# Three groups' first parts are added later on VectorE, their output transfers behind that, and four more blank products run at the start

## The chip, the cores and the metric

The kernel runs on one core of one Trainium2 chip. The metric is the device time of one execution in microseconds, as the median of several runs. The core has five engines that run their own queues in order and wait for each other by semaphores: TensorE (matrix products, PE in the profile), VectorE (DVE), ScalarE (ACT), GpSimd (POOL) and SyncE (SP, which here only starts transfers). A transfer is started by an instruction in one engine's queue and then runs on the DMA engines.

## The reference

An mLSTM cell over 4 batches, 8 heads, 768 steps and 40 features is followed by a feed-forward block on its output, seen as 3072 tokens of 320 features:

```python
for t in range(S):
    m_new = np.maximum(f_gate[:, :, t] + m, i_gate[:, :, t])
    f_stab = np.exp(f_gate[:, :, t] + m - m_new)
    i_stab = np.exp(i_gate[:, :, t] - m_new)
    C = f_stab * C + i_stab * outer(v[t], k[t])
    n = f_stab * n + i_stab * k[t]
    y[:, :, t] = sigmoid(o_gate[t]) * (C @ q[t]) / np.maximum(np.abs(n . q[t]), 1.0)
x = y as (3072, 320)
h = x @ w_in            # 320 -> 2048
g = h - np.tanh(h)
out = g @ w_out         # 2048 -> 320
```

## The kernel before

The sequence is cut into 24 units (6 chunks of 128 steps for each of 4 batches). Two units form a group of 256 tokens, so there are 12 groups, and the feed-forward block works on groups. The 2048 hidden features are 8 pairs of 256 (`p` from 0 to 7). An *item* is one or two pairs of one group: up products into PSUM banks (`ph_up`), then the function g as a polynomial, its *cubes* and products on VectorE with squares on ScalarE, then down products.

**Order.** Every engine's instructions keep the order in which the program issues them (`Pinned`, `T`). The first items are laid out by a planner; from item 7 (`START`) on, a loop lays out one item after another. In it a program clock (`Clock`, line 135) advances by a fixed cost for each product (0.218 for an up product, 0.27 for a down product), and `Clock.later(key, wait, step)` issues a step at the first advance that has passed its due time. This clock only sets the order of the program; it measures nothing.

**Up products in seven.** `up_in_seven` (line 1221) replaces eight block products by seven, on sums of weights and sums of x. Two PSUM banks X and Y hold the partial results; Y's halves are `b` and `e`, X's are `a` and one shared by `c` and `d`. In the order of TensorE: stage one (four products), three down products of an earlier item, stage two (two products), three more down products, stage three (eight products), then the quarter products of the last 64 features. ScalarE copies halves between the products: `b` from `a` and `cs` from `c` behind stage one, `d` from `b` behind stage two, `e` from `b` behind the first product of stage three. The last product of stage three, `w(3)` by `s4`, adds onto `b`. `shrunk` (line 1265) then issues, for ScalarE, a square of `b`, a square of `a`, `q`, `z` and `q`; for VectorE two sums `both` (of `d` and `e` with `cs`) and two cubes. The second `both` waits for the square of `b`. The cubes free the banks for the next item. Behind `shrunk`, by the clock, follow further products, and 3.4 later the sums `s` for the down products (`sums_of_g`, line 1017).

**Put-together.** Down products in seven (`down_seven`, line 1030) collect in PSUM banks `pS`. When a group is done, `put_together` (line 1073) lets ScalarE copy one block (`a`), and its inner `rest` (line 1083), 0.5 later, builds the output tile `ob` on VectorE in four sums. The pairs 0 to 3 of groups 0, 1 and 2 (`g < FIRST`) were done earlier in another way, and their result lies in `parts_of[g]` (128 by 640 numbers); for those, `rest` adds it in a fifth instruction (line 1090). Then the transfer of `ob` to `out` goes into ScalarE's queue, 2.0 later (line 1094).

**Part sums.** `sum_w_in(p)` (line 1197) builds three blocks of sums of weights on GpSimd. For pairs 0, 1 and 2 they are written over `parts_of[p]`, so after that group's add. They are placed at 4.05, 6.05 and 8.05 items behind `START` (line 1737) and are read by the up products of later items (`ph_up<-xT,part`).

**Blank products.** While TensorE has nothing to do at the start, `idle` (line 1698) fills the time with products of a constant into an unused bank (`awake`, line 428). The first stretch, before the first gate transposes, holds ten.

Of the kernel before, what the change touches and what calls it, by code (L numbers as in the profile page):

```python
# [55 lines left out]
OP = mybir.AluOpType  # L56
# [23 lines left out]
def kernel(  # L80
# [33 lines left out]
    V, A, SP, G = Pinned(nc.vector), Pinned(nc.scalar), Pinned(nc.sync), Pinned(nc.gpsimd)  # L114
# [42 lines left out]
    class Plan:  # L157
# [45 lines left out]
        def flow(cls, moved):  # L203
# [22 lines left out]
            return ends  # L226

        def run(self, idle, fill):
            while self.todo:
                ready = [(t, op) for op in self.todo if (t := self.start(op)) is not None]  # L230
# [23 lines left out]
                if op["engine"] == "T":  # L254
                    n = idle(self.free["T"], t)
                    self.done.append((t - n, t, 1.0))
                    us = us * (self.COLD[1] if t < self.COLD[0] else 1.0) + self.TURN * (op["tiles"] != self.tiles)
                    self.tiles = op["tiles"]
                    self.done.append((t, t + us, op["dense"]))
# [21 lines left out]
    GT = 2  # L281
# [12 lines left out]
    FIRST, SPLIT = 3, 4  # L294
# [112 lines left out]
    two = const.tile([128, 1], FP, name="two")  # L407
# [20 lines left out]
    def awake(n):  # L428

        if not spare:  # L430
            spare.append(ps_o.tile([128, 512], FP, name="awake", tag="po1"))
        stream(spare[0], n)

    def stream(bank, n):
        for _ in range(n):
            T.matmul(bank.rearrange("p (h t) -> p h t", h=HH), diag[:, 0], diag[:, 0:1].to_broadcast([128, HH, L]), start=True, stop=True)
# [204 lines left out]
    parts_of = [const.tile([L, GT, DM], FP, name=f"part{g}") for g in range(NP // 2)]  # L641
# [431 lines left out]
    def put_together(g):  # L1073
        bank = pS[g]

        ob = mlp.tile([128, 5, HM], FP, name="ob", tag="ob")
        a = mlp.tile([128, HM], FP, name="a", tag="a", bufs=1)
        u = mlp.tile([128, 2, HM], FP, name="u", tag="u", bufs=1)

        def twice(t):  # L1080
            return t.unsqueeze(1).to_broadcast([128, 2, HM])

        def rest():
            V.tensor_tensor(out=ob[:, 0:5:4], in0=bank[0][:, 0:2], in1=twice(a), op=OP.add)
            V.tensor_tensor(out=u, in0=bank[1], in1=twice(ob[:, 4]), op=OP.add)
            V.tensor_tensor(out=ob[:, 3], in0=bank[1][:, 0], in1=u[:, 1], op=OP.add)
            V.tensor_tensor(out=ob[:, 1:3], in0=bank[2], in1=u, op=OP.add)
            if g < FIRST:
                both = ob[:, 0:2 * GT]
                V.tensor_tensor(out=both, in0=both, in1=parts_of[g].rearrange("p t (two n) -> p (t two) n", two=2), op=OP.add)  # L1090
            c, b = divmod(g * GT, B)
            rows = out.rearrange("(b c t) n -> c t b n", b=B, c=NT)[c][:, b:b + GT]
            whole = ob[:, 0:4].rearrange("p (t two) n -> p t (two n)", two=2)
            Clock.later("sent", 2.0, lambda: A.dma_start(out=rows, in_=whole))

        if g in third:
            return lambda: A.copy(out=a, in_=bank[0][:, 2]), rest
        A.copy(out=a, in_=bank[0][:, 2])
        Clock.later("result", 0.5, rest)
# [97 lines left out]
    def sum_w_in(p, E=V):  # L1197

        a11, a21, a12, a22 = (w_in[:, p, i * 128:(i + 1) * 128] for i in range(4))
        t = sums_in_of(p)  # L1200
        both = w_in[:, p, 0:4 * 128].rearrange("p (j f) -> p j f", j=4)
        return [lambda: E.tensor_tensor(out=t[:, 0:4:2], in0=both[:, 1:4:2], in1=both[:, 0:2], op=OP.subtract),
                lambda: E.tensor_tensor(out=t[:, 1], in0=a22, in1=t[:, 0], op=OP.subtract),
                lambda: E.tensor_tensor(out=t[:, 3], in0=a12, in1=t[:, 1], op=OP.subtract)]
# [196 lines left out]
    while sum(map(len, items)) < len(pairs):  # L1401
        x = sum(map(len, items))
# [18 lines left out]
    plan = Plan(small=("b0", "b1"), a=1, up=1, po0=1, po1=1, gt=2, z=1, s4=1, P=4, vs=4, w64a=2, w64b=2, w=2, wm=2, ob=2)  # L1421
# [45 lines left out]
    of_tokens, of_states, exponentials, rows = {}, {}, [], []  # L1467
# [230 lines left out]
    def idle(t0, t1, share=0.9):  # L1698


        one = 0.43 if t0 < plan.COLD[0] else 0.217
        n = int((t1 - t0) * (1.0 if t0 < plan.COLD[0] else share if t0 > 18.0 or share == 1.0 else 0.65) / one)
        if n and not busy:
            awake(n)
        else:
            pool, tag = next(((pool, tag) for name, pool, tag in (("a", ps_a, "a0"), ("up", ps_h, "ph0"), ("po0", ps_o, "po0"), ("po1", ps_o, "po1"))
                              if plan.tokens[name] and plan.tokens[name][0][0] <= t0), (None, None))
            if n and pool:
                stream(pool.tile([128, 512], FP, name="awake", tag=tag), n)
            else:  # L1710
                n = 0
        return n * one

    plan.run(idle, lambda t0, t1: idle(t0, max(t1, t0 + 0.25), 1.0))


# [3 lines left out]
    def spread_over(steps, x0, x1):  # L1720

        for i, (cost, step) in enumerate(steps):
            at = x0 + i * (x1 - x0) / len(steps)
            work[int(at)].append((at, cost, step))
# [9 lines left out]
    for i, slot in enumerate(slots):  # L1734
        x0, x1 = (START + max(0, 2 * j - 1) for j in (i, i + 1))
        begins[x0].append((slot, x0, x1))
    for p, x in enumerate((4.05, 6.05, 8.05, 2.02, 0.5, 0.8, 1.1, 1.3)):
        spread_over([(0.0, lambda step=step: step()) for step in sum_w_in(p, G)], START + x, START + x + 0.25)
    late = (4, 0.0, V), (5, 0.04, G), (6, 0.95, V), (7, 0.3, G)
    for p, x, E in (*late, *((p, x, G) for p, x in zip(order_of(FIRST)[:2] + order_of(FIRST)[-2:], (1.5, 1.75, 6.6, 7.5)))):  # L1740
# [158 lines left out]
    with tc.If(loaded[0] > 0):  # L1899
# [21 lines left out]
        for g in range(NG):  # L1921
# [18 lines left out]
            ob = [ps_o.tile([128, DM], FP, name="po", tag=f"po{tt}") for tt in range(GT)]  # L1940
# [56 lines left out]
```

## Time and profile before

| what | value |
|---|---|
| median of 3 runs | 492.97 us (492.12 to 493.79) |
| profiled execution | 492.58 us |
| its span, first to last instruction | 490.9 us |
| busy: TensorE, VectorE, ScalarE, GpSimd | 480.2, 409.8, 268.9, 125.3 us |
| mean granted TensorE clock | 0.998 |

Times in rows are microseconds from the start of the span, unless marked ns. In a timeline a row is one instruction or a run of like ones (x4) with its start and length; the brackets give the idle time of the engine before it and what ended that. The ends of products on TensorE are modelled and overlap the next start.

### The profile page before, as it was taken

The page shows a single profiled execution, that of the slowest core. Times are in us where ns is not written, and L with a number is a line of the kernel's source. Part 1 is how long each engine was busy: PE and PEld are TensorE (multiplying, and loading weights), DVE is VectorE, ACT ScalarE, POOL GpSimd, SP SyncE. Part 2 cuts the span into 40 slices and gives each one's busy share as a digit, 9 for nine tenths or more (in the row PEclk, how much of TensorE's full clock was granted, in tenths as well). Part 3 has the DMA queues.
Part 4 walks back from the last instruction along what each step waited for, and adds up shares of the span by engine and source line. Part 5 has one row for each costly group of instructions (what it writes and reads, how often), then busy time and mean ns, then how long its engine had stood idle before and what let it go on. Part 6 is the DMA issues. An engine that isn't in the chain of part 4 may idle for free.

```text
span 490.9 us, 13826 instructions
## 1 busy us (share of the span) xinstructions
PE 480.2 (98%) x5208; PEld 432.5 (88%) x5208; DVE 409.8 (83%) x966; ACT 268.9 (55%) x729; POOL 125.3 (26%) x248
## 2 busy tenths in 40 slices
PE   8999999999899999999999999999999999999995
PEld 4778877789798899999999999999999999998985
DVE  4899989998999997987988888888888888885853
ACT  4888978534445444544644554555455554555540
POOL 5642325827431711111111111102102111111000
PEclk9999999999999999999999999999999999999999
DMA  7996585223635544535544435445345343320001
GB/s 222 308 257 188 75 165 160 72 51 90 144 78 124 114 92 109 115 75 115 109 96 101 97 95 106 103 93 115 68 102 115 79 96 54 65 59 9 28 2 33
DMA packets 140077, 51.27 MB, mean 104 GB/s; under 512 B 119908, under 2 KB 132388, under 8 KB 140004
## 3 DMA queue, kind: packets, MB, share of 16 engines
q1 hardware_dynamic: 131084, 31.18, 31.4%
q0 software_dynamic: 5440, 15.05, 10.6%
q10 hardware_dynamic: 3480, 4.10, 2.5%
q8 instruction: 43, 0.70, 0.6%
q14 instruction: 30, 0.25, 0.2%
HBM read 38.40 MB, written 11.60 MB: 102 GB/s over the span
## 4 chain that ended last, share of the span: by engine, by line
PE 89%; DVE 7%; issue 2%; ACT 1%; DMA 0%; SPq 0%; ACTq 0%; DVEq 0%
PE ph_up L129 39%; PE pS L129 31%; PE po L129 5%; PE pT L129 4%; PE ps L129 3%; PE pc L129 2%; PE ph L129 2%; DVE gt L106 1%; PE awake L129 1%; DVE ob L106 1%; DVE s L106 1%; ACT z L106 1%; DMA w_out<-in_i_gate 0%; DVE both L106 0%; PE px L133 0%
## 5 line engine op out<-in xcount | busy, mean ns | idle before, releaser
L129 PE MATMUL ph_up<-xT,w_in 64*64 64x256 f32 (+3 forms) x1324 | 155.0, 349 | 0.0
L129 PEld LDWEIGHTS ph_up<-xT,w_in 128*128 128x128 f32 (+2 forms) x1324 | 114.0, 162 | 17.2 <-issue 3.3
L106 ACT ACTIVATE z<-ph_up 128x256 f32<-128x256 f32 (+1 forms) x98 | 40.6, 416 | 98.0 <-PE ph_up L129 83.8
L106 POOL DMA_DIRECT2D xT<-y_rows x54 | 31.6, 590 | 238.5 <-DMA y_rows<-yt 218.5
L106 ACT COPY ph_up<-ph_up 128x256 f32<-128x256 f32 x117 | 41.8, 357 | 92.0 <-PE ph_up L129 58.4
L129 PE MATMUL pS<-wT,s 128*128 128x160 f32 x504 | 86.7, 300 | 0.0
L129 PEld LDWEIGHTS pS<-wT,s 128*128 128x128 f32 x504 | 72.9, 191 | 0.3 <-issue 0.3
L106 ACT ACTIVATE q<-z,tiny 128x512 f32<-128x512 f32 (+1 forms) x98 | 68.9, 713 | 2.5
L106 DVE SCALAR_TENSOR_TENSOR gt<-q,gt 128x512 f32<-128x512 f32 (+1 forms) x98 | 66.3, 683 | 3.7 <-ACT q L106 1.2
L106 DVE TENSOR_TENSOR both<-ph_up,cs 128x256 f32<-128x256 f32 x78 | 32.8, 422 | 37.6 <-PE ph_up L129 32.2
L129 PE MATMUL pS<-w_out,gt 128*128 128x160 f32 x336 | 56.9, 312 | 0.0
L129 PE MATMUL ph_up<-xT,sums_in 128*128 128x128 f32 x336 | 51.6, 276 | 2.2 <-DVE gt L106 2.2
L129 PEld LDWEIGHTS pS<-w_out,gt 128*128 128x128 f32 x336 | 46.8, 189 | 4.4 <-issue 1.9
L129 PEld LDWEIGHTS ph_up<-xT,sums_in 128*128 128x128 f32 x336 | 45.5, 191 | 3.2 <-issue 2.6
L129 PE MATMUL ph_up<-xT,part 128*128 128x128 f32 x288 | 44.7, 278 | 1.1 <-DVE gt L106 0.9
L106 DVE SCALAR_TENSOR_TENSOR gt<-ph_up,z 128x256 f32<-128x256 f32 (+1 forms) x98 | 41.1, 457 | 2.3 <-ACT z L106 2.2
L129 PEld LDWEIGHTS ph_up<-xT,part 128*128 128x128 f32 x288 | 38.9, 191 | 2.9 <-ACT ph_up L106 1.8
L106 DVE TENSOR_TENSOR s<-gt 128x256 f32<-128x256 f32 x84 | 33.1, 434 | 1.4
L129 PE MATMUL pS<-wT,gt 128*128 128x160 f32 x168 | 29.8, 300 | 0.0
L129 PE MATMUL pS<-w_out,s 128*128 128x160 f32 x168 | 29.7, 299 | 0.0
L129 PE MATMUL po<-w_out,gt 128*128 128x320 f32 x96 | 27.9, 439 | 0.0
L106 DVE SCALAR_TENSOR_TENSOR gt<-both,z 128x512 f32<-128x512 f32 x39 | 26.6, 683 | 0.0
(141 smaller groups left out, 738.2 us busy)
## 6 DMA issues: line engine op xcount, KB each, us to landing
w<-in_moe_w_out POOLq DMA_DIRECT2D x8, 640.0 KB, 6.1
h_rows<-zt SPq DMA_DIRECT2D x68, 64.0 KB
z_in<-h_rows SPq DMA_DIRECT2D x68, 64.0 KB
w<-in_moe_w_in POOLq DMA_DIRECT2D x16, 256.0 KB, 6.3
kz<-in_kT SPq DMA_DIRECT2D x48, 80.0 KB
o<-in_o_gate SPq DMA_DIRECT2D x24, 160.0 KB
qz<-in_qT SPq DMA_DIRECT2D x44, 80.0 KB
out<-ob ACTq DMA_DIRECT2D x11, 320.0 KB
```

Source lines behind the costliest of these rows:

```text
L106: i = method(*args, **kwargs)
L129: return cls.keep(nc.tensor.matmul(*args, **kwargs))
```

## The change

It does three things. The add of the parts of groups 0, 1 and 2 becomes a step of its own, `add_parts`, due 6.0 after `rest` on the program's clock, and their output transfer is due 1.0 after that; the other groups keep theirs. The first blank stretch gets four more products. The part sums of pairs 0, 1 and 2 move back by 0.2 of an item, so that they are issued after the add that reads what they overwrite.

```diff
@@ put_together, rest @@
             V.tensor_tensor(out=ob[:, 1:3], in0=bank[2], in1=u, op=OP.add)
-            if g < FIRST:
-                both = ob[:, 0:2 * GT]
-                V.tensor_tensor(out=both, in0=both, in1=parts_of[g].rearrange("p t (two n) -> p (t two) n", two=2), op=OP.add)
             c, b = divmod(g * GT, B)
             rows = out.rearrange("(b c t) n -> c t b n", b=B, c=NT)[c][:, b:b + GT]
             whole = ob[:, 0:4].rearrange("p (t two) n -> p t (two n)", two=2)
-            Clock.later("sent", 2.0, lambda: A.dma_start(out=rows, in_=whole))
+
+            def add_parts():
+                both = ob[:, 0:2 * GT]
+                V.tensor_tensor(out=both, in0=both, in1=parts_of[g].rearrange("p t (two n) -> p (t two) n", two=2), op=OP.add)
+                Clock.later("sent", 1.0, lambda: A.dma_start(out=rows, in_=whole))
+
+            if g < FIRST:
+                Clock.later("sent", 6.0, add_parts)
+            else:
+                Clock.later("sent", 2.0, lambda: A.dma_start(out=rows, in_=whole))
@@ idle @@
-            awake(n)
+            awake(n + 4 if t0 < plan.COLD[0] else n)
@@ places of sum_w_in @@
-    for p, x in enumerate((4.05, 6.05, 8.05, 2.02, 0.5, 0.8, 1.1, 1.3)):
+    for p, x in enumerate((4.25, 6.25, 8.25, 2.02, 0.5, 0.8, 1.1, 1.3)):
```

## Rows read from the trace of the kernel before

**Rows 1.** The page, chain of work that ended last, shares by engine.

```profile
PE 89%; DVE 7%; issue 2%; ACT 1%; DMA 0%; SPq 0%; ACTq 0%; DVEq 0%
```

**Rows 2.** Waits of TensorE: who waited for whom, us in total, times, longest.

```profile
PE ph_up L129 <- DVE gt L106: 3.1, 3, 1.8
...
PE ph_up L129 <- ACT ph_up L106: 0.2, 1, 0.2
```

**Rows 3.** TensorE's timeline: start, us, what, idle before; the three restarts and `w(3)` products.

```profile
130.20 0.68 PE L129 MATMUL ph_up<-xT,sums_in 128*128 128x128 f32 x4 [1.77 <-DVE gt L106]
...
134.58 1.63 PE L129 MATMUL ph_up<-xT,w_in 128*128 128x128 f32 x20
...
150.23 0.68 PE L129 MATMUL ph_up<-xT,part 128*128 128x128 f32 x4 [0.91 <-DVE gt L106]
...
154.62 1.63 PE L129 MATMUL ph_up<-xT,w_in 128*128 128x128 f32 x20
...
169.76 0.68 PE L129 MATMUL ph_up<-xT,sums_in 128*128 128x128 f32 x4 [0.40 <-DVE gt L106]
...
174.23 1.63 PE L129 MATMUL ph_up<-xT,w_in 128*128 128x128 f32 x20
```

**Rows 4.** VectorE's timeline behind group 0's put-together, and group 2's add.

```profile
127.06 0.82 DVE L106 TENSOR_TENSOR ob<-ob,part 128x640 f32<-128x640 f32 x1
127.80 0.48 DVE L106 TENSOR_TENSOR vs<-v,crossed 128x320 f32<-128x320 f32 x1
...
128.97 0.42 DVE L106 TENSOR_TENSOR both<-ph_up,cs 128x256 f32<-128x256 f32 x1 [0.35 <-ACT z L106]
129.31 0.75 DVE L106 SCALAR_TENSOR_TENSOR gt<-ph_up,z 128x256 f32<-128x256 f32 x2
...
166.47 1.03 DVE L106 TENSOR_TENSOR ob<-ob,part 128x640 f32<-128x640 f32 x1
```

**Rows 5.** ScalarE's timeline: group 0's transfer, the next square, the copy `e` from `b`.

```profile
127.92 0.44 ACTq L106 DMA_DIRECT2D out<-ob  x1
128.46 0.38 ACT L106 ACTIVATE z<-ph_up 128x256 f32<-128x256 f32 x1 [4.72 <-DVE vs L106]
...
133.89 0.36 ACT L106 COPY ph_up<-ph_up 128x256 f32<-128x256 f32 x1 [0.86 <-PE ph_up L129]
```

**Rows 6.** Timelines of ScalarE and VectorE, one item later: squares and sums `both`.

```profile
136.37 0.38 ACT L106 ACTIVATE z<-ph_up 128x256 f32<-128x256 f32 x1 [2.12 <-PE ph_up L129]
...
137.64 0.71 DVE L106 TENSOR_TENSOR both<-ph_up,cs 128x256 f32<-128x256 f32 x2
...
156.40 0.38 ACT L106 ACTIVATE z<-ph_up 128x256 f32<-128x256 f32 x1 [2.12 <-PE ph_up L129]
...
156.54 0.79 DVE L106 TENSOR_TENSOR both<-ph_up,cs 128x256 f32<-128x256 f32 x2
```

**Rows 7.** VectorE's timeline: the last of the sums `s` behind group 1's put-together.

```profile
154.59 0.43 DVE L106 TENSOR_TENSOR s<-gt,s 128x256 f32<-128x256 f32 x1
```

**Rows 8.** Timelines of GpSimd and VectorE: part sums of pair 0, sums `s`.

```profile
133.02 1.16 POOL L106 TENSOR_TENSOR part<-w_in 128x256 f32<-128x256 f32 x1
134.26 1.11 POOL L106 TENSOR_TENSOR part<-w_in,part 128x128 f32<-128x128 f32 x2
...
133.64 1.42 DVE L106 TENSOR_TENSOR s<-gt 128x256 f32<-128x256 f32 x2
```

**Rows 9.** Timeline of TensorE's products (PE) and loads (PEld) in the first 12 us.

```profile
1.14 3.86 PE L129 MATMUL awake<-diag 128*128 128x512 bf16 x10 [1.14 <-DVE probe L106]
...
3.67 0.15 PEld L129 LDWEIGHTS <-diag 128*128 128x128 bf16 x1 [0.28 <-issue]
...
4.10 0.15 PEld L129 LDWEIGHTS <-diag 128*128 128x128 bf16 x1 [0.28 <-issue]
...
5.46 0.28 PE L133 MATMUL gate<-ident,w_in 32*128 32x32 f32 x2 [0.46 <-DVE w_in L106]
...
7.51 1.24 PE L129 MATMUL awake<-diag 128*128 128x512 bf16 x5
...
9.78 2.12 PE L129 MATMUL awake<-diag 128*128 128x512 bf16 x9
```

## The prediction

> **What bounds the kernel now.** The chain of work that ended last comes first: 89% of it is TensorE, 7% VectorE [rows 1]. So a microsecond counts if TensorE loses or gains it. The waits of TensorE say where it stands still: three waits for VectorE's cubes make up nearly all of its idle time behind the first microseconds, and one short wait for a ScalarE copy is left [rows 2]. The timeline of TensorE places the three: at 130.20, 150.23 and 169.76 [rows 3], each where the next item's up products begin, just behind the put-together of groups 0, 1 and 2, which are the groups that the change edits. Their listed idle times are 1.77, 0.91 and 0.40 us, 3.08 in all; the ends of products are modelled, so the true waits are a little longer.
>
> VectorE's and ScalarE's timelines there show why. Group 0's parts are added at 127.06; only then come `vs`, the two sums `both` and the two cubes, which end at 129.31 + 0.75 = 130.06, and TensorE starts 0.14 later [rows 3, 4]. The add takes 0.74 of that queue (127.80 - 127.06). It costs a second time: the output transfer stands in ScalarE's queue ahead of the next square and waits there for the add. It issues at 127.92, ScalarE has stood 4.72 when its square starts at 128.46 [rows 5], and the second `both` loses 0.35 to that square [rows 4]. Where nothing holds the square, the second sum starts 0.71 - 0.42 = 0.29 behind the first (137.64, [rows 6]); here it starts 0.35 + 0.42 = 0.77 behind, so 0.48 is lost.
>
> **The change part by part: what goes.** Without add and transfer there, group 0's cubes end 0.74 + 0.48 = 1.22 earlier, at 128.84. Group 1 has the same rows 20.03 later, and its cubes end at 150.23 - 0.14 = 150.09, so 148.87. Group 2's add is 1.03 long and overlaps what follows by 0.08 as group 0's does (127.06 + 0.82 - 127.80), so 0.95 goes [rows 4]: 169.62 becomes 168.67. If this were all, TensorE would gain 1.22 + 0.91 + 0.40 = 2.5 us.
>
> **What comes back: where the two moved steps land.** `rest` is issued five products of 0.218 and a step of 1.5 before `shrunk`, 2.59 on the program's clock. The next sums come 3.4 behind `shrunk`, at 5.99, the add at 6.00: so right behind them on VectorE, whose queue goes on with `o`, `ys` and `yt`. From there the clock counts one down product (0.27), two up products (0.44, the copy `d` from `b`), two down products: at 1.25 it issues the transfer, due at 1.0. One down and two up products later, at 1.95, follows the copy `e` from `b`. So on ScalarE the transfer passes the two squares, `q`, `z`, `q` and three copies, and stops **one instruction ahead of the copy `e` from `b`**. ScalarE waits in it for the add, the add stands behind the sums, and behind ScalarE's wait TensorE waits: `w(3)` by `s4` adds onto `b`, which that copy must have read. In the trace that copy runs at 133.89, its product at 134.58 [rows 3, 5], while VectorE's sums end only some 5 us behind the cubes. Nothing in between covers the wait.
>
> Its price: from cubes to the end of the sums 155.02 - 150.09 = 4.93 where GpSimd does not disturb (154.59 + 0.43, [rows 7]); the add, 0.74 of place beyond them; from its end to ScalarE's next instruction 128.46 - 127.88 = 0.58 [rows 4, 5]; the copy 0.36; TensorE 0.05 behind it (an estimate from the 0.04 to 0.05 between dependent instructions in these timelines). Sum 6.66 from the end of the cubes to the product.
>
> Block 0: 128.84 + 6.66 = 135.50 against 134.58 before: +0.92, although the up products began 1.22 earlier.
> Block 1: TensorE's quarters, which ended at 134.58 + 1.63 = 136.21, now end 0.92 later, and so does ScalarE's square behind them: 136.37 becomes 137.29. VectorE's pair, which was at 137.64 by its own queue, now starts with the square, 0.35 earlier than before [rows 3, 6]. Group 1's cubes: 148.87 - 0.35 = 148.52. TensorE comes to the up products at 150.23 - 0.91 + 0.92 = 150.24, so it waits there no more: the first loss has eaten the second gain. The product: 148.52 + 6.66 = 155.18 against 154.62: +0.56.
> Block 2: the square 156.40 becomes 156.96 and holds VectorE's pair, before at 156.54: +0.42 [rows 6]. Cubes 168.67 + 0.42 = 169.09. TensorE wants them at 169.76 - 0.40 + 0.56 = 169.92, no wait. The product: 169.09 + 6.66 = 175.75 against 174.23: **+1.52**. Behind it TensorE has no gap but the 0.2 that [rows 2] show, so this stays to the end.
>
> **The part sums on GpSimd** start later: they overwrite the parts, so they wait for the add, and the new 4.25, 6.25 and 8.25 put them behind it in program order. The rest of GpSimd's queue is passed by nothing; behind them wait the loads of `xT`, which need `y_rows`, themselves later. The sums use 1.16 + 1.11 us [rows 8] and are read an item or more later: nothing on the path. The output itself lands some 7 us later; nobody reads it. What they disturb moves: in group 0 two of VectorE's `s` take 1.42 beside them [rows 8]; from the cubes' end to the next `both` it is 137.64 - 130.06 = 7.58 there and 156.54 - 150.09 = 6.45 in group 1 [rows 4, 6], so 1.13 is lost to GpSimd. Now it falls on `o`, `ys` and `yt` behind the add: add end 134.51, 1.5 of work (155.02 to 156.54), 1.13, so 137.14, just before the 137.29 of TensorE's side. It is covered by 0.15.
> There the Trainium skill speaks against the change: "SBUF — State Buffer", Who interferes with whom, says that a VectorE instruction with two SBUF inputs and a GpSimd one that reads SBUF hold the shared port pair in turn, each for its whole length. By that the stretch could lose all 2.27 and not the 1.13 of the row; that is rival 2.
>
> **The four blank products.** The first stretch has ten from 1.14 to 5.00; the first gate transposes wait 0.46 for VectorE and start at 5.46. The loads of the first ones lie 0.43 apart (3.67, 4.10), 512 columns at the lower clock level, 1.2 GHz, though the mean granted clock reads 0.998; in later stretches nine take 2.12 and five 1.24, so 0.22 each, the upper level of 2.4 GHz, with a modelled tail of 0.14 behind the last [rows 9]. The last of the ten are at the upper level, since ten at 0.43 would take 4.3 and not 3.86. Four more then end at 1.14 + 3.86 + 0.88 - 0.14 = 5.74: the first transposes move by some 0.25, those behind (which waited for VectorE as well) by about 0.1. I take +0.1. After the 0.46 pause the clock did not fall (the next blanks are at the upper level), so no row shows a gain. Both sides: 0 if a later wait covers it, a gain of up to 0.46 if other executions lose that pause to the clock; 4 x 0.43 = 1.7 lost if all four run at the lower level.
> On this the Trainium skill, "TensorE: Matmul & The Clock Gate", What's actually happening, says that one kernel can have 6, 11 or 14 slow products at its start from run to run. This trace has seven or eight, (4.10 - 1.14) / 0.43 and the one that starts there; what others have no run here shows, and rival 3 takes it up.
>
> **Sum.** +1.52 + 0.1 = +1.6 us. The profiled execution took 492.58 (span 490.9 and 1.7 around it), so 494.2 of its kind; it lies 0.39 under the median of 492.97, which gives **494.6**, 0.33% slower. A difference of 0.3%, 1.48 us, is about what a measurement tells from none, so the forecast lies on that border. Its own range: if VectorE keeps its old times in block 2, cubes at 168.67, it is +1.1, and 494.0; each block hands its error to the next, so 0.15 to 0.3 more in each makes +2.4, and 495.4.
>
> **Rivals.**
> 1. The transfer does not hold TensorE, because ScalarE goes past it or the product need not wait for the copy. Then only the gains are left: -2.5 + 0.1, 490.6, faster. Against it: ScalarE's 4.72 us behind the same transfer [rows 5], and TensorE waiting for a ScalarE copy in [rows 2]. It decides where the copy `e` from `b` starts before the add has ended.
> 2. GpSimd's part sums hold VectorE for their whole 2.27: `both` in block 0 comes at 134.51 + 1.5 + 2.27 = 138.28, +0.64; cubes 149.51, product 156.17, +1.55. In block 1 add end 155.18, `both` 158.95, +2.41; cubes 171.08, product 177.74: +3.5, 496.6. Against it: the 1.13.
> 3. In usual executions the clock rises later than here, and the fourteen blanks run at the lower level: they end at 1.14 + 14 x 0.43 = 7.16, which holds the transposes 1.7 and not 0.1: 494.6 + 1.6 = 496.2. For it: the three runs lie 1.7 us apart; against it, this trace.
> That the change does nothing is no rival: the order on both queues is fixed by the program.
>
> **How the numbers follow.** The forecast gets 0.70 (0.38 above +0.3%, 0.32 within), rival 1 0.14, rival 2 0.09, rival 3 0.07. So slower 0.38 + 0.09 + 0.07 = 0.54, same 0.32, faster 0.14. The range runs from 491.8, which leaves out rival 1 and little else, to 496.6, with both slow rivals at its upper end.
>
> **What would show it.** Right: the three waits for the cubes shrink to one of some 0.7 at 129; ScalarE's transfer issues just behind the add and its copy `e` from `b` starts 0.1 after it; TensorE shows three new waits for ScalarE's `ph_up` of about 2.1, 0.6 and 1.2. VectorE's second `both` has no wait for a square. Wrong: those three waits are missing or below 0.5 (rival 1), `o` and `yt` beside GpSimd take twice their length (rival 2), or the first transposes come after 6 us (rival 3).

## The result, and the profile after

The changed kernel takes **495.91 us** in the median of 22 executions (495.27 to 497.91), the kernel before, beside it, 493.43 (492.12 to 498.65). The ratio is **1.004, with a 95% interval from 1.0022 to 1.0059**: slower by some 2 us (2.5 by the medians). The forecast was 494.6 with a range from 491.8 to 496.6. The profiled execution of after took 496.64 (span 494.9); most of the 22 lie between 495.3 and 496.2, and the profiled one is longer by a fall of the clock that is shown below. Of the 109 executions of the kernel before in all comparisons 24 took over 496.5 us, mostly some 498.4, against a usual 493.5, so its medians stand a little above its usual time.

The waits of TensorE (who waited for whom: us in total, times, longest) and the chain's shares by engine are, in after:

```profile
PE ph_up L129 <- ACT ph_up L106: 3.3, 2, 1.8
...
PE ph_up L129 <- POOL part L106: 1.0, 1, 1.0
...
PE ph_up L129 <- DVE gt L106: 0.5, 1, 0.5
...
PE 88%; DVE 4%; DMA 2%; SPq 1%; ACT 1%; issue 1%; POOL 0%; ACTq 0%; DVEq 0%
```

Against [rows 2], 3.1 us of waiting for cubes (`gt`) have become 0.5, and the 0.2 of other waits has become 4.3. VectorE's share of the chain fell from 7% to 4% [rows 1], and the kernel became slower all the same. TensorE's timeline places the waits:

```profile
129.49 0.68 PE L129 MATMUL ph_up<-xT,sums_in 128*128 128x128 f32 x4 [0.47 <-DVE gt L106]
...
135.92 2.15 PE L129 MATMUL ph_up<-xT,w_in 128*128 128x128 f32 x20 [1.76 <-ACT ph_up L106]
...
157.72 1.71 PE L129 MATMUL ph_up<-xT,w_in 128*128 128x128 f32 x20 [1.05 <-POOL part L106]
...
178.41 1.74 PE L129 MATMUL ph_up<-xT,w_in 128*128 128x128 f32 x20 [1.57 <-ACT ph_up L106]
```

The restart behind group 0 comes 0.71 earlier than in [rows 3] (129.49 against 130.20), although TensorE arrived some 0.5 later from the start. Then the product `w(3)` by `s4` comes 1.34, 3.10 and 4.18 later than 134.58, 154.62 and 174.23. ScalarE's timeline shows what held it:

```profile
132.09 0.36 ACT L106 COPY ph_up<-ph_up 128x256 f32<-128x256 f32 x1 [0.54 <-ACT cs L106]
135.03 0.44 ACTq L106 DMA_DIRECT2D out<-ob  x1
135.51 0.36 ACT L106 COPY ph_up<-ph_up 128x256 f32<-128x256 f32 x1 [3.06 <-DVE o L106]
...
156.76 0.41 ACTq L106 DMA_DIRECT2D out<-ob  x1
157.22 0.36 ACT L106 COPY ph_up<-ph_up 128x256 f32<-128x256 f32 x1 [2.26 <-DVE o L106]
```

The copy `d` from `b` (132.09) is done, the transfer is next in ScalarE's queue, and it issues at 135.03. Only then runs the copy `e` from `b`, and 0.05 behind its end TensorE goes on. In what follows this wait is called a hold. The label "GpSimd part" at 157.72 hides one of the same kind. That start follows the copy too (157.22 + 0.36 = 157.58), though by 0.14 and not by 0.05, just as GpSimd's first part sum of that group ends (157.71). In e3 below the same product starts before that sum has begun, so it does not need it; what makes the 0.09 between is open. VectorE's timeline says for what the transfer waited:

```profile
134.18 0.82 DVE L106 TENSOR_TENSOR ob<-ob,part 128x640 f32<-128x640 f32 x1
134.92 0.48 DVE L106 TENSOR_TENSOR o<-o,den 128x320 f32<-128x320 f32 x1
135.44 1.23 DVE L106 TENSOR_TENSOR ys<-z_in,o 128x256 f32<-128x256 f32 x2
...
138.17 0.96 DVE L106 TENSOR_TENSOR both<-ph_up,cs 128x256 f32<-128x256 f32 x2 [0.90 <-PE ph_up L129]
```

The add ends at 134.18 + 0.82 = 135.00, the transfer issues 0.03 later. Last come the windows (stretch, length, busy time and instructions of TensorE, its loads, VectorE, ScalarE, GpSimd, granted clock, DMA share, GB/s):

```profile
135.00:137.10 2.10, 1.18 (x16) 0.93 (x20) 2.03 (x6) 0.36 (x1) 1.86 (x3) 1.00 0.63 224
137.10:140.53 3.43, 3.43 (x68) 2.99 (x62) 2.31 (x8) 2.26 (x8) 0.01 (x1) 0.50 0.24 40
140.53:142.00 1.47, 1.47 (x22) 1.42 (x20) 1.15 (x4) 1.11 (x2) 0.00 (x0) 1.00 0.18 29
```

Behind the wait of 1.76 the granted clock is at its lower level, 1.2 GHz (0.50), for 3.43 us, though TensorE is busy all the while, and then at 2.4 GHz again. TensorE's lateness grows from 1.34 to about 3.0 in it. e2 below shows the same holds without such a fall. That most executions of after have none either is inferred from their times and their mean granted clocks, mostly 0.997 to 1.0 against 0.994 here.

### The profile page after: what moved, and what is told of

It reads as the page before. It is cut to its first block, busy times and chain, and to the rows that moved or that the text cites. A ratio compares the mean times of both kernels' runs of the same rounds, so it can differ in the third digit from the quotient of the medians.

```text
span 494.9 us, 13827 instructions
## 1 busy us (share of the span) xinstructions
PE 483.5 (98%) x5212; PEld 434.8 (88%) x5212; DVE 411.6 (83%) x966; ACT 268.9 (54%) x729; POOL 125.7 (25%) x248
## 4 chain that ended last, share of the span: by engine, by line
PE 88%; DVE 4%; DMA 2%; SPq 1%; ACT 1%; issue 1%; POOL 0%; ACTq 0%; DVEq 0%
PE ph_up L129 38%; PE pS L129 30%; PE po L129 5%; PE pT L129 4%; PE ps L129 3%; PE pc L129 2%; PE awake L129 2%; PE ph L129 2%; SPq L106 1%; DMA z_in<-h_rows 1%; DVE gt L106 1%; DVE s L106 1%; DMA h_rows<-zt 1%; DVE ob L106 1%; ACT z L106 1%
```

## The experiments

In each, "net of the start" means that the shift of TensorE against the trace of before is taken without the shift that it already had from the start of the kernel. Differences come from the starts of the same row in both traces.

**e1: the blanks alone, on the kernel before.**

```diff
-            awake(n)
+            awake(n + 4 if t0 < plan.COLD[0] else n)
```

> The kernel before with the four more blank products and nothing else of the change. Theory of the hold (the transfer in ScalarE's queue costs what was lost): 0 to +0.6 us against before; the three waits of TensorE for the cubes stay at 1.8, 0.9 and 0.4. Rival (the blanks carry the loss): +1.5 us or more.

Measured: 493.92 (493.49 to 494.72, 12 executions) against 493.90, ratio 0.999 (0.9961 to 1.0019). In its trace TensorE is 0.35 late from 9 us on. The median of the kernel before counts its long executions too; against its usual time in this comparison, 493.6, the blanks cost 0.3. Their other side comes with e5. The waits for the cubes are 1.76, none and 0.82, not 1.8, 0.9 and 0.4: behind the first one the clock falls (last section), TensorE's lateness grows from 0.35 to 1.99, and the second wait is gone.

**e2: the changed kernel with ten blanks.**

```diff
-            awake(n + 4 if t0 < plan.COLD[0] else n)
+            awake(n)
```

> The changed kernel with ten blank products as before. Theory of the hold: 0 to 0.6 us faster than the changed kernel, so +1.4 to +2.4 us against before, with three waits of TensorE for ScalarE's copy of 1.0 to 1.8. Rival (the blanks): within 0.5 us of before.

Measured: 495.44 (494.99 to 500.68, 12 executions), ratio 1.0045 (1.0005 to 1.0085); its profiled execution took 495.20, 2.62 more than that of before, and holds no fall of the clock. TensorE's timeline:

```profile
129.02 0.68 PE L129 MATMUL ph_up<-xT,sums_in 128*128 128x128 f32 x4 [0.46 <-DVE gt L106]
...
135.45 1.74 PE L129 MATMUL ph_up<-xT,w_in 128*128 128x128 f32 x20 [1.75 <-ACT ph_up L106]
...
155.64 1.71 PE L129 MATMUL ph_up<-xT,w_in 128*128 128x128 f32 x20 [1.04 <-POOL part L106]
...
176.54 1.74 PE L129 MATMUL ph_up<-xT,w_in 128*128 128x128 f32 x20 [1.69 <-ACT ph_up L106]
```

It is 0.11 early from the start, so net of that the three products come 0.98, 1.13 and 2.42 later than in [rows 3]. The three holds make nearly the whole slowdown, 2.42 of 2.73 net of the start. This trace serves for the sums of the next section.

**e3: the transfer one instruction further back.** The add stays where the change puts it; the transfer is due 2.0 and not 1.0 behind it, which moves it past the copy `e` from `b` on ScalarE and past nothing else.

```diff
-                Clock.later("sent", 1.0, lambda: A.dma_start(out=rows, in_=whole))
+                Clock.later("sent", 2.0, lambda: A.dma_start(out=rows, in_=whole))
```

> The changed kernel with the transfers due 2.0 and not 1.0 behind the add: on ScalarE they then stand one instruction later, behind the copy e from b, and nothing else moves. Theory of the hold: the waits of TensorE for that copy go, what is left is the gain, -2.5 us with up to +0.6 for the blanks, so -1.5 to -2.5 us against before (491 to 492) and about 4 us faster than the changed kernel. Rival (GpSimd's part sums beside VectorE cost it): at least 1 us slower than before, less than 1 us faster than the changed kernel.

Measured: 492.41 (491.17 to 493.49, 12 executions), ratio **0.9951 (0.9918 to 0.9983)**, 3.5 us below after. The timelines of TensorE, ScalarE and, for one row, GpSimd:

```profile
129.09 0.68 PE L129 MATMUL ph_up<-xT,sums_in 128*128 128x128 f32 x4 [0.46 <-DVE gt L106]
...
152.67 1.63 PE L129 MATMUL ph_up<-xT,w_in 128*128 128x128 f32 x20
...
165.51 1.35 PE L129 MATMUL pS<-w_out,gt 128*128 128x160 f32 x8 [0.48 <-DVE ob L106]
...
168.83 0.68 PE L129 MATMUL ph_up<-xT,sums_in 128*128 128x128 f32 x4 [0.68 <-DVE gt L106]
```

```profile
132.91 0.36 ACT L106 COPY ph_up<-ph_up 128x256 f32<-128x256 f32 x1 [0.86 <-PE ph_up L129]
134.63 0.44 ACTq L106 DMA_DIRECT2D out<-ob  x1
135.40 0.38 ACT L106 ACTIVATE z<-ph_up 128x256 f32<-128x256 f32 x1 [2.12 <-PE ph_up L129]
```

```profile
154.07 0.91 POOL L106 TENSOR_TENSOR part<-w_in 128x256 f32<-128x256 f32 x1 [8.03 <-DVE ob L106]
```

The copy runs at 132.91, as soon as its product is there, and the transfer waits behind it, in time in which ScalarE has nothing else: the square behind the transfer waited for TensorE. No wait for a ScalarE copy is left. In group 1 the product `w(3)` by `s4` starts at 152.67, before GpSimd's part sum at 154.07, which the label in after's row named. One place in one queue is worth 3.5 us and the sign. But the gain against before is 1.5 (493.9 to 492.4) and not the 2.5 of the full sum: net of the start, the trace is 1.33 ahead at the restart behind group 0 and some 2.2 behind group 1, and has given half of it back behind group 2 (1.1 at the product that stood at 184.08 before). There TensorE waits 0.48 and 0.68 for VectorE, which still does the add, only later; ahead of its work, TensorE meets VectorE's queue again.

**e4: only the transfer moved, on the kernel before.** The add stays ahead of the cubes; the transfer of the three groups goes behind the squares.

```diff
-            Clock.later("sent", 2.0, lambda: A.dma_start(out=rows, in_=whole))
+            Clock.later("sent", 3.0 if g < FIRST else 2.0, lambda: A.dma_start(out=rows, in_=whole))
```

> The kernel before with the add where it was, and only the transfers of groups 0 to 2 due 3.0 and not 2.0 behind rest, so that they stand behind the squares on ScalarE. Theory (the add costs twice, 0.74 by its place on VectorE and 0.48 by the square behind the transfer): 0.48 goes at each of the three waits, 0.4 in the last: -1.3 us, with waits for the cubes of about 1.3, 0.4 and 0. Rival (the add's place alone counts, or the later transfer holds another copy): 0 or above.

Measured: 491.89 (490.99 to 497.61, 12 executions), ratio **0.9944 (0.9902 to 0.9987)**; profiled 491.18 against 492.58. TensorE's restarts:

```profile
130.01 0.68 PE L129 MATMUL ph_up<-xT,sums_in 128*128 128x128 f32 x4 [1.33 <-DVE gt L106]
...
149.90 0.68 PE L129 MATMUL ph_up<-xT,part 128*128 128x128 f32 x4 [0.62 <-DVE gt L106]
```

The wait of 1.77 becomes 1.33: 0.44 for group 0, where the working had put 0.48 on the transfer. In group 1 0.91 becomes 0.62, and in group 2 no wait for cubes is left. The transfer alone gives as much as e3. The two differ in the blanks as well, but e9 below, with e3's fourteen, comes to the same ratio, 0.9950 against 0.9951. The gain is above the 1.3 that was expected. In the trace 0.65 of it (0.90 net of the start) is there at the product that stood at 184.08, and the profiled execution is 1.40 shorter; where the rest comes from was not followed up. Taking the add out of the cubes' way brings nothing more by the end, since the work on VectorE stays.

**e5 and e8: fewer and more blanks**, on the kernel before: six (`awake(n - 4 ...)`) and twelve (`awake(n + 2 ...)`).

> The kernel before with six and not ten blank products at the start, so that TensorE stands still from about 3.7 to 5.4 us. In the runs so far, kernels with ten blanks had executions some 5 us longer than the rest (8 of 35 of the kernel before), kernels with fourteen had none (0 of 46). Theory (in those executions TensorE's clock rises late, since the pause falls before the rise): with six blanks the long execution becomes the usual one, +4 to +6 us against before's usual 493, and the trace shows products at the lower level, 0.43 apart, well behind 5 us. Rival (the long executions come from elsewhere): the same two kinds of times as before, about 493 most often.

> The kernel before with twelve blanks. Theory (blanks cost only what they run beyond 5.46 us, and keep the clock if they leave no pause): two more end at about 5.3, so no change of the usual time, 493 to 493.6, and none or few of the executions some 5 us longer. Rival (it takes fourteen): the same share of long executions as before, one in four.

Measured, e5: 496.35 (494.69 to 498.17, 9 executions) against 493.69, ratio 1.0026 (0.9989 to 1.0063); e8: 493.59 (492.71 to 494.56, 12 executions), ratio 0.9976 (0.9946 to 1.0005). TensorE's first microseconds in e5:

```profile
1.14 2.74 PE L129 MATMUL awake<-diag 128*128 128x512 bf16 x6 [1.14 <-DVE probe L106]
5.35 0.39 PE L133 MATMUL gate<-ident,w_in 32*128 32x32 f32 x2 [1.47 <-DVE w_in L106]
...
8.83 2.34 PE L129 MATMUL awake<-diag 128*128 128x512 bf16 x5
...
13.12 3.93 PE L129 MATMUL awake<-diag 128*128 128x512 bf16 x9
```

Six blanks at 1.2 GHz end 1.47 before the transposes can start. Behind that pause the five blanks that took 1.24 in [rows 9] take 2.34, and the nine that took 2.12 take 3.93, with their loads 0.43 apart: they run at the lower level, to some 16.8 us, where before leaves it by about 4.5. (This is read from the spacing; the profile's clock column reads 1.00 there.) What began at 11.73 in before begins 5.15 later; this execution took 498.15. The median is only 2.7 above before's, below the 4 to 6 expected, so the pause does not cost 5 us each time, and what decides it is open. With twelve or fourteen blanks and no holds (e1, e3, e7, e8, e9, e10) none of 72 executions was over 494.72, while the kernel before with its ten has the 24 long ones, and e2, also with ten, has three at 500.5 to 500.7. None of these was profiled; that they are a late rise behind the pause of 0.46 [rows 9] is inferred from e5, whose profiled execution is longer by the same 5 us.

**e6: a longer hold.** In the changed kernel VectorE does one more instruction of the add's size ahead of each of the three adds.

```diff
+                V.tensor_tensor(out=both, in0=both, in1=both, op=OP.max)
                 V.tensor_tensor(out=both, in0=both, in1=parts_of[g].rearrange("p t (two n) -> p (t two) n", two=2), op=OP.add)
```

> The changed kernel with one more VectorE instruction of the add's size (a maximum of ob with itself, which changes no number) ahead of each add, some 0.82 to 0.86 us. Theory of the blocks that hand on (each hold also delays VectorE's next pair, and so the next group's cubes): +0.85 behind the first group, +1.7 behind the second, +2.5 behind the third against the changed kernel, 498 to 499. Rival (only the last hold counts, the earlier ones are absorbed by TensorE's slack): +0.85, about 496.8.

Measured: 500.99 (500.55 to 501.67, 4 executions), ratio 1.0124 (1.0065 to 1.0184). TensorE's timeline:

```profile
1.14 5.85 PE L129 MATMUL awake<-diag 128*128 128x512 bf16 x14 [1.14 <-DVE probe L106]
...
137.50 1.74 PE L129 MATMUL ph_up<-xT,w_in 128*128 128x128 f32 x20 [2.60 <-ACT ph_up L106]
...
158.54 1.71 PE L129 MATMUL ph_up<-xT,w_in 128*128 128x128 f32 x20 [1.90 <-POOL part L106]
...
180.32 2.89 PE L129 MATMUL ph_up<-xT,w_in 128*128 128x128 f32 x20 [2.55 <-ACT ph_up L106]
```

Each wait grows by about 0.86 against e2. In this execution the start already cost 1.34; net of it the products are 1.58, 2.58 and 4.75 late, and against e2's 0.98, 1.13 and 2.42 that is 0.60, 1.45 and 2.33 for one, two and three extra instructions. Each block hands its loss on whole: that part of the working stands. The time is above what I expected: the clock falls behind the last, long hold, from 180.6 to 184.0 (TensorE's lateness grows from 6.09 to 7.82, so 1.7 more), and all four executions show a mean granted clock of 0.990 to 0.996, where e2's are mostly at 0.997 to 1.0.

**e7: the add on GpSimd**, in the place of e3, with twelve blanks.

```diff
-                V.tensor_tensor(out=both, in0=both, in1=parts_of[g]..., op=OP.add)
-                Clock.later("sent", 1.0, lambda: A.dma_start(out=rows, in_=whole))
+                G.tensor_tensor(out=both, in0=both, in1=parts_of[g]..., op=OP.add)
+                Clock.later("sent", 2.0, lambda: A.dma_start(out=rows, in_=whole))
```

> A version meant to be better than both: the add of the parts on GpSimd in place of VectorE, the transfers behind the copy e from b as in the run with the transfer one copy later, and twelve blanks. Theory (VectorE's queue is what remains, as there are still waits of 0.5 and 0.7 for its cubes): 0.5 to 1.3 us less than with the transfer behind the copy (492.4), 491 to 492, no wait for ScalarE's copy. Rival (GpSimd's add disturbs VectorE as much as it relieves it): the same as there, 492.4, or above.

Measured: 493.25 (492.22 to 494.62, 12 executions), ratio 0.9965 (0.9938 to 0.9993), above the 491 to 492 expected and no better than e3. GpSimd's and TensorE's timelines:

```profile
132.80 1.55 POOL L106 TENSOR_TENSOR ob<-ob,part 128x640 f32<-128x640 f32 x1
```

```profile
150.03 0.71 PE L129 MATMUL ph_up<-xT,part 128*128 128x128 f32 x4 [0.73 <-POOL xT L106]
```

The add takes 1.55 there, twice VectorE's, and GpSimd's own sums of `xT` come late: TensorE waits for them, 0.73 here and 1.20 at 341 us, and two waits of 0.5 for the cubes stay. (The profiled execution, 494.62, is the longest of the twelve.) VectorE is relieved of the add, and TensorE waits for the next queue.

**e9 and e10: e4 with fourteen and with twelve blanks.**

> A version meant to be better than both kernels: the add of the parts where it was before, the transfers of groups 0 to 2 behind the squares (as in the run that moves the transfers alone), and fourteen blanks as in the change. Theory (the two effects add): the usual time of that run, 491.8, with 0.3 to 0.6 for the blanks, so 492.1 to 492.4, and no execution some 5 us longer. Rival (the later start of everything meets other waits): 493 or above.

> The same with twelve blanks, which end about when the first transposes can start. Theory: 491.8 to 492.3, and no execution some 5 us longer, as with twelve blanks alone. Rival (twelve are too few in some executions): one or two of twelve some 5 us longer.

Measured: e9 492.60 (491.44 to 494.21), ratio 0.9950 (0.9918 to 0.9982); e10 **492.34** (491.37 to 492.75), ratio **0.9934 (0.9902 to 0.9967)**, 12 executions each, against 494.16; both medians lie just above what was expected. e10 keeps TensorE's waits for cubes of e4, 1.33 and 0.67, and has no execution above 492.75: the version that beats both kernels.

## Why the prediction was right in sign and short in size

**What goes: right.** Group 0's cubes were to end 1.22 earlier. In e2 TensorE restarts at 129.02 against 130.20, 1.18 earlier, 1.07 net of the start. It waits 0.46 there, where 0.7 was named, and no more in groups 1 and 2, as said.

**Where the transfer lands: right, and it decides.** It stops one instruction ahead of the copy `e` from `b`, as counted from the program's clock, and e3, in which only that place differs, is 3.5 us faster. So rival 1 was the right picture of a kernel one queue place away. Its size was not: it counted 2.5, and e3 and e4 give 1.5 and 2.0 by medians (each against the kernel before measured beside it), for the add stays on VectorE's queue and group 2 gives gain back.

**The price of the hold: right.** From the cubes' end to the product 6.66 was worked out. In e2 these rows of VectorE hold the cubes ahead of the three holds (`gt` from `ph_up`), with the instructions that the last part of this section needs:

```profile
137.31 0.96 DVE L106 TENSOR_TENSOR both<-ph_up,cs 128x256 f32<-128x256 f32 x2 [0.51 <-PE ph_up L129]
...
146.54 0.75 DVE L106 TENSOR_TENSOR vs<-v,crossed 128x320 f32<-128x320 f32 x1
147.30 0.42 DVE L106 TENSOR_TENSOR both<-ph_up,cs 128x256 f32<-128x256 f32 x1
147.91 0.42 DVE L106 TENSOR_TENSOR both<-ph_up,cs 128x256 f32<-128x256 f32 x1 [0.18 <-ACT z L106]
148.25 0.75 DVE L106 SCALAR_TENSOR_TENSOR gt<-ph_up,z 128x256 f32<-128x256 f32 x2
...
163.43 1.64 DVE L106 TENSOR_TENSOR s<-gt 128x256 f32<-128x256 f32 x2
...
169.29 0.74 DVE L106 SCALAR_TENSOR_TENSOR gt<-ph_up,z 128x256 f32<-128x256 f32 x2
```

In group 1 the cubes end at 149.00 and the product comes at 155.64, 6.64 later; in group 2 170.03 and 176.54, 6.51; in group 0 the cubes end about 0.14 ahead of the restart, 128.88, and the product comes 6.57 later. The listed waits, 1.75, 1.04 and 1.69, stand against 2.1, 0.6 and 1.2.

**The step that failed: what a block hands to the next.** Products were to be late by 0.92, 0.56 and 1.52; net of the start they are by 0.98, 1.13 and 2.42. Block 0 holds. Then the working let VectorE's whole stretch up to the next cubes move with its pair `both`, whatever runs beside it. From product 0 to the cubes of group 1 that made 148.52 - 135.50 = 13.02, and e2 has 149.00 - 135.45 = 13.55; from product 1 to the cubes of group 2 it made 169.09 - 155.18 = 13.91, and e2 has 170.03 - 155.64 = 14.39. So each handing-on was 0.5 short. The rows above say where. The pair `both` starts at 137.31, as forecast. Its second sum now meets the square that starts with it, and the pair takes 0.96 in place of 0.71 [rows 6], but this costs little, since a wait behind it is gone that before had:

```profile
139.32 0.69 DVE L106 SCALAR_TENSOR_TENSOR gt<-q,gt 128x512 f32<-128x512 f32 x1 [0.30 <-ACT q L106]
```

In e2 the same product follows without a wait, 1.73 behind the pair's start and not 1.68. The loss comes further on: `vs` takes 0.75 in place of 0.48 (in [rows 4], and in group 1 of before too), beside GpSimd's sums of `xT` (146.49, 1.12), which wait for TensorE and so came later than before. And the second `both` of group 1 still waits 0.18 for its square, now because TensorE's products are later, and starts 0.61 behind the first where 0.29 was taken. "No wait for a square" was wrong there. In group 2's stretch the two sums `s` take 1.64 where they took 0.96 before, beside GpSimd's sums of `wT`. An instruction that moves against another engine does not keep its length. The working's own allowance, 0.15 to 0.3 more in each block and +2.4 at the end, had room for this, but gave no reason for it.

**The blanks: mis-sized.** 0.1 was taken. In after the fourteen are done at 5.7, as worked out, and what follows the first transposes is 0.08 late, as taken (7.59 against the 7.51 of [rows 9]):

```profile
1.14 4.59 PE L129 MATMUL awake<-diag 128*128 128x512 bf16 x14 [1.14 <-DVE probe L106]
5.66 0.31 PE L133 MATMUL gate<-ident,w_in 32*128 32x32 f32 x2
...
7.59 1.24 PE L129 MATMUL awake<-diag 128*128 128x512 bf16 x5
...
10.02 2.12 PE L129 MATMUL awake<-diag 128*128 128x512 bf16 x9
```

Then it is 0.24 late (10.02 against 9.78) and 0.5 by 124 us; what held it there is open. In e1 the same fourteen take 4.87, as more of them run at the lower level (loads 0.43 apart up to 4.53 us, in after up to 3.67), and it is 0.35 late. Starts with ten blanks differ as much, from 0.11 early (e2) to 0.25 late (e4), so no single trace prices the blanks. The usual times say 0.3 (e1) to 0.7 (after against e2 without its three long executions, 495.25). And "a gain if other executions lose that pause to the clock" was kept as a bound only, for want of a row; the executions with twelve and fourteen blanks speak for it (e5, e8), though in after it does not outweigh the holds.

**The sum again.** 494.6 with 2.42 for 1.52 and 0.35 for 0.1 becomes 495.75; after is at 495.91. That it comes so close is in part luck: the forecast stood on 492.97, the median of three runs, and the kernel before took 493.43 beside after. On that base the same terms give 496.2.

**Rival 2** falls. Beside the part sums of after the two `ys` take 1.23 (135.44, above), against 0.56 in group 1 of before, where nothing disturbs them:

```profile
135.09 0.90 POOL L106 TENSOR_TENSOR part<-w_in 128x256 f32<-128x256 f32 x1 [2.04 <-DVE ob L106]
136.06 1.05 POOL L106 TENSOR_TENSOR part<-w_in,part 128x128 f32<-128x128 f32 x2
```

```profile
155.45 0.56 DVE L106 TENSOR_TENSOR ys<-z_in,o 128x256 f32<-128x256 f32 x2
```

So the disturbance is there; but `both` then waits for TensorE, 0.90 in the profile after and 0.51 in e2. It is covered, by more than the 0.15 of the working. The Trainium skill, "SBUF — State Buffer", Who interferes with whom, has whichever of the two engines issues first hold the shared port pair for its whole instruction. Rival 2 made of this that VectorE loses all of GpSimd's time; of the part sums' 0.90 + 1.05 the rows show 0.67 lost, and here it was free.

**Rival 3** is half true. In e6 the fourteen blanks end at 7.0 (its row above), as it said, and the start costs 1.34; in after the same fourteen end at 5.7. The Trainium skill, "TensorE: Matmul & The Clock Gate", What's actually happening, says that the number of slow products at the start differs from run to run; these two traces agree. As the usual case it does not stand: it needs 1.7 for the blanks, and e2's usual time is only 0.7 below after's.

**What no rival had**: that a hold can cost a second time, by the clock behind it. It gives 1.7 where it stands in after's profile, of which 1.2 is left at the third product (4.18 less 0.53 of the start, against e2's 2.42), and 1.7 in e6's last block. It is an extra of some executions, not the cause: e2's trace has the full loss without it.

## What to carry to other kernels

A transfer that waited for another engine's result held, in these runs, every instruction behind it on the queue that starts it (ScalarE stood 3.06 us in after); look for what follows it there, and for who waits for that, and put it where the queue would stand idle anyway. One place further back turned this change from 0.4% slower into 0.5% faster, and moving the transfer alone, with the add left in place, gave all of it. When TensorE gains time against two other engines, work out anew what will run beside what: an engine's stretch does not move as a block.

## What the runs showed of the hardware that was not expected

- Behind a wait of 1.76 us in the middle of dense work the granted clock fell to 0.50 for 3.43 us while TensorE was busy throughout (after, 137.10 to 140.53). It was so behind a wait of 2.55 in e6 (180.6 to 184.0), and around group 0's wait in e1 (130.9 to 134.3). Behind the wait of 1.75 in e2's profile and the 1.77 of [rows 3] it was not. The waits were equal and the outcome was not; what decides it stays open.
- Behind a pause of 1.47 us ahead of the clock's first rise, products ran at the lower level to some 16.8 us (e5's profiled execution). With two blanks more than before, none of the 12 executions of e8 was above 494.56; TensorE is 0.39 late at 107 us in its profile. The mean granted clock does not show the late rise: e5's profile reads 0.998.
